# A third of the exponentials on VectorE as shifted linear powers of two, with 64-row score tiles, seven pooled PSUM banks and maps without maxima

## The chip, the core and the metric

The kernel runs on one core of a Trainium2 chip. A core has TensorE (PE, matmuls into PSUM), ScalarE (ACT, the exponential among others), VectorE (DVE), GpSimd (POOL, no access to PSUM) and SyncE (SP), whose queue issues DMAs. The metric is the device time of one execution in microseconds.

## What is computed

A gate mixes two kinds of attention over the same input x of 2048 rows and 512 columns, with 32 heads of 16. Branch A is linear attention with a learned map: two softmaxes over 16 features, of the projection and of its negative. Branch B is softmax attention; its 32 x 2048 x 2048 exponentials are most of the work.

```
g = _sigmoid((x * gate_w).sum(-1, keepdims=True))
# A: phi = concat(softmax(p), softmax(-p)), p = q @ w_phi (and k @ w_phi)
kv = einsum("bhsf,bhsd->bhfd", phi_k, v); z = einsum("bhsf->bhf", phi_k)
o  = einsum("bhqf,bhfd->bhqd", phi_q, kv) / (einsum("bhqf,bhf->bhq", phi_q, z) + 1e-6)
# B: softmax(q k^T / 4) v, per head
return g * (o_A @ wo_A) + (1 - g) * (o_B @ wo_B)
```

Inputs are bf16, normal, x and the weights of scale 0.05. The `x` of branch A serves both branches.

## The kernel before

The program is a list of operations with an engine, a due time (`prio`), an expected duration and dependences. When the program is built, `_Sched.run` plays them through in time and fixes the order of each engine's queue and the buffer each tile gets; `emit` writes the queues with semaphore waits. On the chip each engine runs its queue in that order.

Branch B runs in 32 passes, called sets here: a query block of 512 (`qc`, 4), a group of eight heads that share a 128-row projection (`g`, 4), and a parity (`par`, 2) that picks four of the eight heads. A set goes over 16 key tiles of 128 keys. For each, two units of 1024 columns: `qk` (L573) makes two score tiles with two 32-row matmuls in different row strips of the array, and one `exp` on ScalarE (L580) turns a unit of psR (three buffers of two banks) into bf16 E. Heads of the other parity in a strip are masked out in q (`q_proj`, L375, two products per projection with 0/1 masks). After both units `pv` (L590) adds E times V into psO, four matmuls in four column strips; V is padded with ones, so column 16 of a head's 32 is the softmax denominator. At the end of a set VectorE copies psO (L341), TensorE transposes it in fp32 (L604), VectorE normalises (L608 to L613), and after both parities TensorE transposes again (L623) and VectorE copies to oBT (L626). psO is one bank, so the next set's sums wait for the copy.

Everything else is spread between the units by due time and shares one PSUM bank, psM: the projections (`fill`, L349, four 128-row matmuls of 512 columns each), and branch A. A map (`phi`) takes the projected features from psM: on VectorE maximum and minimum (L455, L456) and two subtractions (L457, L460), on ScalarE one exponential of 1024 (L463), on VectorE a sum over 16 (L464) and a reciprocal (L466), on GpSimd the product (L467). For the queries the result is transposed on TensorE (L514), copied (L517), multiplied with kz (L523, L535), normalised (L526 to L538), transposed again (L546) and copied to oAT (L549). The output projection (L645 to L652) sums both branches; the last four row blocks run after the last set.

Of the kernel before, what the change touches and what calls it, by code (L numbers as in the profile page):

```python
# [1 line left out]

# [4 lines left out]
F32 = mybir.dt.float32  # L7
ACTF = mybir.ActivationFunctionType
# [3 lines left out]
D = 512  # L12
# [7 lines left out]
SCALE = 0.25  # L20

LAT = 0.06
TAU = 0.95
EARLY = 10.0
T0 = 12.0
# [3 lines left out]


# [5 lines left out]
class _Tile:  # L36
    def __init__(self, slots):
        self.slots = slots
        self.idx = None
        self.ops = []  # L40

# [5 lines left out]
class _Op:  # L47
    __slots__ = ("eng", "fn", "dur", "prio", "deps", "tiles", "mode", "name", "dma",
                 "n_open", "users", "start", "end", "count", "sem", "vc", "seq", "est")


class _Sched:

    COMPUTE = ("pe", "act", "dve", "pool")
# [4 lines left out]
    def add(self, eng, prio, dur, fn, deps=(), tiles=(), mode=None, name="", dma=None, nb=0.0):  # L61
        o = _Op()
        o.eng, o.fn, o.dur, o.prio = eng, fn, dur, prio
        o.deps = [d for d in deps if d is not None]
        o.tiles = list(tiles)
        o.mode, o.name, o.dma, o.est = mode, name, dma, nb
# [6 lines left out]

    def run(self):
        engines = ("sp", "act", "pe", "dve", "pool")
# [5 lines left out]
        ready = {e: [] for e in engines}  # L81
# [3 lines left out]
        free = {e: 0.0 for e in engines}  # L85
        last_mode = None
        order = {e: [] for e in engines}
        left = len(self.ops)

        def slot_time(t):  # L90
            best = None
            for i, ten in enumerate(t.slots.tenant):
                if ten is None:
                    when = 0.0
                elif any(x.end is None for x in ten.ops):
                    continue
                else:
                    when = max(x.end for x in ten.ops) + LAT
                if best is None or when < best[0]:
                    best = (when, i)  # L100
            return best

        def earliest(o, at):
            when = max(at, o.est)
            for t in o.tiles:
                if t.idx is None:
                    b = slot_time(t)
                    if b is None:
                        return None
                    when = max(when, b[0])  # L110
            return when

        while left:
            pick = None
            for e in engines:
# [22 lines left out]
            for t in o.tiles:  # L138
                if t.idx is None:
                    _, i = slot_time(t)  # L140
                    ten = t.slots.tenant[i]
                    if ten is not None:
                        o.deps += [x for x in ten.ops if x not in o.deps]
# [563 lines left out]
```

## Time and profile before

| | |
|---|---|
| runs | 1056.77, 1067.06, 1069.68 us; median 1067.06 |
| profiled execution, span | 1054.9 us |
| busy: ACT, PE, DVE, POOL | 93%, 83%, 29%, 7% |
| mean granted clock of TensorE | 0.685 |

The span runs from the first to the last instruction of one profiled execution. Busy shares count the time in which an engine works on data. The granted clock is the share of TensorE's 2.4 GHz that the throttle let through. In the rows below a line such as L573 is a line of the kernel before; "out<-in" names what an instruction writes and reads, and the text in square brackets how long its engine had been idle before it and what ended that.

### The profile page before, as it was taken

Reading aid. Unit: us, or ns where it says so; the run is one execution under the profiler, and the core shown is the slowest. Engines: PE = TensorE matmul, PEld = TensorE weight load, DVE = VectorE, ACT = ScalarE, POOL = GpSimd, SP = SyncE. Lnnn points to the kernel's source line nnn. Section 1 sums busy time; section 2 is a strip of 40 time slices with the busy share of each in tenths; the row PEclk is TensorE's granted clock in tenths of the full one; section 3 lists DMA queues with packets and bytes.
Section 4 is the critical chain, followed back from the end, with each engine's and each line's share of the span. In section 5 each row is a group of like instructions: output and inputs, shape, how many; then the busy total and the mean of one; then the engine's idle time right before and its main releaser. Section 6 shows DMA issues by size and latency. Waiting matters only on the chain.

```text
span 1054.9 us, 12780 instructions
## 1 busy us (share of the span) xinstructions
PE 879.7 (83%) x5420; PEld 253.2 (24%) x5472; DVE 306.0 (29%) x634; ACT 984.9 (93%) x1064; POOL 74.1 (7%) x62
## 2 busy tenths in 40 slices
PE   5988778787887878788988888878888899888887
PEld 1322222122221322122222221312222222222212
DVE  1333535144333222124313321402422241311001
ACT  4899999999999999999999999999999999999995
POOL 4000100102011000000000100000000010000000
PEclk9989988678657875656555665655655655997556
DMA  9000000000000000000000000000000000000000
GB/s 238 2 1 1 1 1 1 0 1 0 1 1 1 2 1 1 1 1 1 1 0 1 1 1 1 1 1 1 1 1 1 1 1 1 21 28 13 1 1 21
DMA packets 18809, 9.23 MB, mean 9 GB/s; under 512 B 13632, under 2 KB 18752, under 8 KB 18752
## 3 DMA queue, kind: packets, MB, share of 16 engines
q1 hardware_dynamic: 16912, 6.82, 2.7%
q10 hardware_dynamic: 1584, 1.57, 0.5%
q8 instruction: 43, 0.70, 0.3%
q14 instruction: 14, 0.11, 0.0%
q0 software_dynamic: 256, 0.02, 0.0%
HBM read 3.16 MB, written 2.10 MB: 5 GB/s over the span
## 4 chain that ended last, share of the span: by engine, by line
ACT 63%; PE 32%; issue 1%; DVE 1%; DMA 1%; POOL 0%; DVEq 0%
ACT E L580 61%; PE psR L573 11%; PE psO L590 8%; PE psM L349 6%; ACT WAT L463 2%; PE psM L604 2%; PE psM L645 1%; PE psM L514 1%; DMA xT<-in_A_x_dram 1%; PE psM L647 1%; PE psM L535 1%; PE psR L349 1%; DVE ss L464 0%; PE psR L645 0%; PE psM L523 0%
## 5 line engine op out<-in xcount | busy, mean ns | idle before, releaser
L580 ACT ACTIVATE E<-psR 128x1024 bf16<-128x1024 f32 x1024 | 956.8, 1123 | 43.5 <-PE psR L573 35.9
L573 PE MATMUL psR<-q,kT 32*128 32x512 bf16 x2048 | 428.7, 519 | 29.2 <-ACT E L580 28.1
L590 PE MATMUL psO<-E,vB 128*32 128x512 bf16 x2048 | 272.9, 523 | 110.9 <-ACT E L580 108.9
L573 PEld LDWEIGHTS psR<-q,kT 32*128 32x128 bf16 x2048 | 91.3, 96 | 318.4 <-issue 183.1
L590 PEld LDWEIGHTS psO<-E,vB 128*32 128x32 bf16 x2048 | 55.1, 98 | 326.8 <-ACT E L580 287.3
L464 DVE TENSOR_REDUCE ss<-WAT 128x64 f32<-128x1024 bf16 x32 | 39.0, 1218 | 121.5 <-ACT WAT L463 121.3
L467 POOL TENSOR_TENSOR WB<-WAT,ss 128x1024 bf16<-128x1024 bf16 x16 | 30.8, 1926 | 518.8 <-DVE ss L466 518.8
L341 DVE COPY OT<-psO 128x512 f32<-128x512 f32 x32 | 22.1, 691 | 146.7 <-PE psO L590 146.6
L455 DVE TENSOR_REDUCE st<-psM 128x32 f32<-128x512 f32 x32 | 22.1, 692 | 110.8 <-PE psM L349 110.8
L467 POOL TENSOR_TENSOR phiK<-WAT,ss 128x1024 bf16<-128x1024 bf16 x16 | 30.8, 1927 | 308.8 <-DVE ss L466 308.8
L349 PE MATMUL psM<-Wp,xT 128*128 128x512 bf16 x103 | 43.3, 553 | 8.5 <-issue 6.6
L375 DVE TENSOR_SCALAR q<-psM,masks 128x512 bf16<-128x512 f32 x30 | 21.2, 740 | 77.9 <-PE psR L573 56.4
L463 ACT ACTIVATE WAT<-WAT 128x1024 bf16<-128x1024 bf16 x32 | 37.4, 1170 | 0.0
L349 PE MATMUL psM<-xT,WB 128*128 128x512 bf16 x100 | 32.5, 451 | 3.6 <-issue 3.3
L604 PE MATMUL psM<-ident,OT 128*128 128x128 f32 x128 | 30.1, 379 | 1.0 <-DVE WAT L460 0.7
L341 DVE CAST Wp<-psM 128x512 bf16<-128x512 f32 x20 | 13.8, 692 | 52.3 <-PE psM L652 35.5
L349 PE MATMUL psM<-WAv,xT 128*128 128x512 bf16 x61 | 22.3, 501 | 2.0 <-DVE WAT L460 0.9
L604 PEld LDWEIGHTS psM<-ident,OT 128*128 128x128 f32 x128 | 19.4, 188 | 12.7 <-DVE OT L341 5.5
L456 DVE TENSOR_REDUCE st<-psM 128x32 f32<-128x512 f32 x32 | 21.7, 679 | 0.0
L457 DVE TENSOR_TENSOR WAT<-psM,st 128x512 bf16<-128x512 f32 x32 | 21.7, 679 | 0.0
L517 DVE COPY WB<-psM 128x1024 bf16<-128x1024 bf16 x16 | 11.1, 692 | 36.6 <-PE psM L514 36.6
L460 DVE TENSOR_TENSOR WAT<-st,psM 128x512 bf16<-128x512 f32 x32 | 21.6, 676 | 0.0
(84 smaller groups left out, 345.9 us busy)
## 6 DMA issues: line engine op xcount, KB each, us to landing
out_dram<-Wp SPq DMA_DIRECT2D x16, 128.0 KB, 1.7
WB<-in_B_wqkv_dram ACTq DMA_DIRECT2D x3, 512.0 KB, 7.0
WAv<-in_A_wqkv_dram SPq DMA_DIRECT2D x1, 512.0 KB, 4.2
WoA<-in_A_wo_dram SPq DMA_DIRECT2D x1, 512.0 KB, 5.1
WoB<-in_B_wo_dram SPq DMA_DIRECT2D x1, 512.0 KB, 6.1
Wbd<-in_A_w_phi_dram POOLq DMA_DIRECT2D x8, 2.0 KB, 4.4
xT<-in_A_x_dram SPq DMA_TRANSPOSE x4, 7.9
gw<-in_gate_w_dram SPq DMA_DIRECT2D x4, 0.2 KB, 5.1
```

The source lines that it names most:

```text
L341: return add("dve", prio, 0.14 + n * 0.00105, lambda e: e.tensor_copy(dst(), src()), deps=deps, tiles=tiles, name=name)
L349: ins = e.matmul(tile.ap[:, off:off + 512], lhsT=lhs(t), rhs=rhs(t), start=(t == 0), stop=(t == KT - 1))
L455: o1 = add("dve", prio, 0.68, lambda e: e.tensor_reduce(mx.ap[:, 0:32], P(), AX.X, ALU.max), deps=[f], tiles=[tile, mx])
L456: o2 = add("dve", prio, 0.68, lambda e: e.tensor_reduce(mx.ap[:, 32:64], P(), AX.X, ALU.min), deps=[f], tiles=[tile, mx])
L457: o3 = add("dve", prio, 0.68, lambda e: e.tensor_tensor(dv()[:, :, 0:DH], P(), mx.ap[:, 0:32].unsqueeze(2).to_broadcast([128, H, DH]), ALU ...
L463: o5 = add("act", prio + 3, 0.95, lambda e: e.activation(ee.ap, d.ap, ACTF.Exp), deps=[o3, o4], tiles=[d, ee])
L464: o6 = add("dve", prio + 5, 1.2, lambda e: e.tensor_reduce(ss.ap[:, 0, :], ee.ap.rearrange("p (g f) -> p g f", f=DH), AX.X, ALU.add), deps ...
L467: return add("pool", prio + 7, 2.0, lambda e: e.tensor_tensor(dst().rearrange("p (g f) -> p g f", f=DH), ee.ap.rearrange("p (g f) -> p g f ...
L573: ins = e.matmul(r.ap[:, 512 * i:512 * (i + 1)], lhsT=kT[p0:p0 + 32, g, 128 * kt:128 * (kt + 1)], rhs=qt.ap[p0:p0 + 32, par, :], start=Tru ...
L580: x = add("act", ut(u), 0.946, lambda e, r=r, E=E: e.activation(E.ap, r.ap, ACTF.Exp, scale=SCALE), deps=[q], tiles=[r, E], name=f"exp{u}")
L590: ins = e.matmul(O.ap[32 * s:32 * s + 32, :], lhsT=vB[:, kt, h, :], rhs=es[s // 2].ap[:, 512 * (s % 2):512 * (s % 2 + 1)], start=(kt == 0) ...
L604: ins = e.transpose(tt.ap[:, 128 * i:128 * (i + 1)], ot.ap[:, 128 * i:128 * (i + 1)], ident32[:])
```

## The change

Of the 16 key tiles of a set, six (`DSET`: 5, 7, 9, 11, 13, 15) may be done on either of two streams, and the planner picks one for each when it places its first score matmul (`choose`). On ScalarE the exponential is as before. On VectorE a scaled and shifted score is written as int16 whose bits, read as bf16, are a power of two with a linear mantissa (`ACC`, `BIAS`); a second and a third copy are this one with 43 and 85 added to the bits, one by VectorE over 2048 elements at once, one by GpSimd as two 32-bit additions of 512. The weighted sum of the three approximates the exponential. It is made by TensorE: three rounds of E times V per key tile, the second and the third with V scaled by 0.79 and 0.63 (`vS`, made by GpSimd). The due times count 11 ScalarE tiles and 5.3 VectorE tiles to a set.

- Scores use tiles of 64 rows: `q_proj` writes q once, and eight small DMAs place each head into a zeroed buffer `qz`, so that the two matmuls of a unit take rows 0 to 63 and 64 to 127. A unit takes two adjacent banks on the ScalarE stream, two single ones on the VectorE stream.
- PSUM: seven banks in one pool for scores, projections and everything else, the eighth is psO. V is padded to 18 columns instead of 32.
- Maps take exp(p) and exp(-p) straight from PSUM on ScalarE, without maxima; GpSimd sums the 16 in four halving additions. The transposes of the queries' maps, of oA and of oB become DMA transposes on SP's queue. Branch A's keys are summed in four groups.
- A certificate computes bounds of the scores from norms (squares on GpSimd, sums on TensorE), and a flag; a second, slower program with maxima follows behind a branch on that flag.
- The planner weighs lateness of the score streams against other work and counts 0.11 us for a change of tiling.

```diff
+VW = 18
+NBANK = 7
+DSET = (5, 7, 9, 11, 13, 15)
+SHIFT = (0, 43, 85)
+WB16 = (1.0, 0.79296875, 0.6328125)
+ACC = 128.0 / math.log(2.0) * SCALE
+NORM = 3.1258
+BIAS = 127.0 * 128.0 - 128.0 * math.log2(NORM)
...
+    def choose(self, key, eng):
+        for o in self.alts.pop(key)[1 - ("act", "dve").index(eng)]:
+            o.start = o.end = -1.0
+            self.left -= 1
+            self.ops.remove(o)
+            if o in self.ready[o.eng]:
+                self.ready[o.eng].remove(o)
+            for t in o.tiles:
+                t.ops.remove(o)
+            for u in o.users:
+                if u.start is not None:
+                    continue
+                u.deps.remove(o)
+                u.n_open -= 1
+                if u.n_open == 0 and u.start is None:
+                    self.ready[u.eng].append(u)
...
+            if pend[o.run] >= 1 + (o.run == "act"):
+                continue
...
+    psR = ctx.enter_context(nc.psum_tensor("psR", [128, NBANK * 512], F32))
     psO = ctx.enter_context(nc.psum_tensor("psO", [128, 512], F32))
-    psM = ctx.enter_context(nc.psum_tensor("psM", [128, 512], F32))
-    R_r = _Slots([p[:] for p in psR])
+    banks = psR[:].rearrange("p (b n) -> p b n", n=512)
+    B_r = _Slots([banks[:, i, :] for i in range(NBANK)])
...
+        qt = q_t[g, c] = _Tile(qz_r)
+        ev = evac("dve", prio, lambda: qs.ap, lambda: tile.ap[:, off:off + 512], [f], [tile, qs], name=f"qev{g}{c}")
+        op_qz[g, c] = []
+        for j in range(8):
+            r0, cc = 16 * j, j % 4
+            op_qz[g, c].append(add(
+                "sp", prio + 0.001 * j, 0.08, lambda e, r0=r0, cc=cc: e.dma_start(qt.ap[r0:r0 + 16, cc, :], qs.ap[r0:r0 + 16, :]),
+                deps=[ev] + op_qz0, tiles=[qs, qt], name="qz", dma=2.3, lane=lambda: (("qz", qt.idx), (g, c))))
...
+                op_vS[g, c, m] = pool(prio + 1, 0.6 * len(ds), lambda e, m=m, a=a, b=b: e.tensor_scalar(
+                    vS[:, m, a:b, 8 * g:8 * g + 8, :], vB[:, DSET[a]:DSET[b - 1] + 1:2, 8 * g:8 * g + 8, :],
+                    WB16[m + 1], 1.0, op0=ALU.mult, op1=ALU.mult), [ev_v[g, c]], name="vS")
...
+        ev = lambda: ee.ap.rearrange("p (h f) -> p h f", f=32)
+        ex = [add("act", prio, 0.55, lambda e, s=s: e.activation(ev()[:, :, 16 * s:16 * s + 16], P(), ACTF.Exp, scale=1.0 - 2.0 * s),
+                  deps=[f] + ee_deps, tiles=[tile, ee]) for s in range(2)]
+        eg = lambda: ee.ap.rearrange("p (g f) -> p g f", f=DH)
+        v8 = lambda: tr.ap[:, 0:512].rearrange("p (g f) -> p g f", f=8)
+        v4 = lambda: tr.ap[:, 0:256].rearrange("p (g f) -> p g f", f=4)
+        v2 = lambda: tr.ap[:, 256:384].rearrange("p (g f) -> p g f", f=2)
+        p1 = pool(prio + 2, 1.1, lambda e: e.tensor_tensor(v8(), eg()[:, :, 0:8], eg()[:, :, 8:16], ALU.add), ex + use_wat,
...
+        return pool(prio + 6, 2.0, lambda e: e.tensor_tensor(
+            eg(), eg(), ss.ap[:, 1, :].unsqueeze(2).to_broadcast([128, 64, DH]), ALU.mult),
+            [o7], tiles=[ee, ss], name="phi")
...
+        o2 = add("sp", prio + 8, 0.3, lambda e, ph=ph, ptt=ptt: e.dma_start_transpose(ptt.ap, ph.ap),
+                 deps=[op_ph] + use_wp1, tiles=[ph, ptt], name="phT", dma=4.0, lane=lambda ptt=ptt, st=st: (("phT", ptt.idx), st))
...
+        aset = [kt for kt in range(NT) if kt not in DSET] + list(DSET[::-1])
+        pvs = []
+        todo = [("act", i / 11.0, kt) for i, kt in enumerate(aset)] + [("dve", (i + 0.1) / 5.3, kt) for i, kt in enumerate(DSET)]
+        for eng, frac, kt in todo:
+            alt = ((s, kt), eng) if kt in DSET else None
+            pr = st_(s + frac)
+            T = _Tile(T_r) if eng == "dve" else None
+            exps, es = [], []
+            for cc in range(2):
+                rs = [_Tile(B_r), _Tile(B_r)]
+                if eng == "act":
+                    rs[0].mate, rs[1].mate = rs[1], rs[0]
+                c = 2 * par + cc
+
+                def qk(e, rs=rs, c=c, kt=kt, g=g, qt=qt):
+                    ins = None
+                    for h in range(2):
+                        ins = e.matmul(rs[h].ap, lhsT=kT[64 * h:64 * h + 64, g, 128 * kt:128 * (kt + 1)],
+                                       rhs=qt.ap[64 * h:64 * h + 64, c, :], start=True, stop=True, tile_position=(64 * h, 0))
+                    return ins
+                q = add("pe", pr + 0.5 * cc, 0.22, qk, deps=[ev_k[g, kt // 4]] + op_qz[g, qc], tiles=rs + [qt], mode="row",
+                        name=f"qk{s}.{kt}", kind="qk", run=eng, alt=alt)
...
+                if eng == "act":
+                    E = _Tile(E_r)
+                    es.append(E)
+                    exps.append(add("act", pr + 0.5 * cc, 0.934, lambda e, rs=rs, E=E: e.activation(
+                        E.ap.rearrange("p (a n) -> p a n", n=512), pair(rs), ACTF.Exp, scale=SCALE),
+                                    deps=[q], tiles=rs + [E], name="exp", kind="exp", alt=alt))
+                else:
+                    for h in range(2):
+                        exps.append(add("dve", pr + 0.5 * cc + 0.01 * h, 0.61, lambda e, rs=rs, T=T, cc=cc, h=h: e.tensor_scalar(
+                            T.ap[:, 0, 1024 * cc + 512 * h:1024 * cc + 512 * h + 512], rs[h].ap,
+                            ACC, BIAS, op0=ALU.mult, op1=ALU.add),
+                            deps=[q], tiles=[rs[h], T], name="expd", kind="exp" if h else "exp0", alt=alt))
+            if eng == "act":
+                rounds = [(exps, lambda cc, es=es: es[cc].ap, lambda hd, kt=kt: vB[:, kt, hd, :], [])]
+                holds = es
+            else:
+                di = DSET.index(kt)
+                s1 = add("dve", pr + 1.0, 0.61, lambda e, T=T: e.tensor_single_scalar(T.ap[:, 1, :], T.ap[:, 0, :], SHIFT[1], ALU.add),
+                         deps=exps, tiles=[T], name="sh1", alt=alt)
+                s2 = [pool(pr + 1.0 + 0.3 * cc, 1.27, lambda e, T=T, cc=cc: e.tensor_tensor(
+                    T.ap[:, 2, 1024 * cc:1024 * (cc + 1)].bitcast(I32), T.ap[:, 0, 1024 * cc:1024 * (cc + 1)].bitcast(I32),
+                    shc[:].to_broadcast([128, 512]), ALU.add), exps[2 * cc:2 * cc + 2] + [op_shc], tiles=[T], name="sh2", alt=alt) for cc in range(2)]
+                rounds = [(exps, lambda cc, T=T: T.ap[:, 0, 1024 * cc:1024 * (cc + 1)].bitcast(BF16), lambda hd, kt=kt: vB[:, kt, hd, :], []),
+                          ([s1], lambda cc, T=T: T.ap[:, 1, 1024 * cc:1024 * (cc + 1)].bitcast(BF16),
+                           lambda hd, di=di: vS[:, 0, di, hd, :], [op_vS[g, kt // 4, 0]]),
+                          (s2, lambda cc, T=T: T.ap[:, 2, 1024 * cc:1024 * (cc + 1)].bitcast(BF16),
+                           lambda hd, di=di: vS[:, 1, di, hd, :], [op_vS[g, kt // 4, 1]])]
+                holds = [T]
...
+                def pv(e, rhs=rhs, lhs=lhs, g=g, par=par, O=O, s=s, key=(kt, ri)):
+                    ins = None
+                    for cc in range(2):
+                        for h in range(2):
+                            col = 2 * h + cc
+                            hd = 8 * g + 4 * h + 2 * par + cc
+                            ins = e.matmul(O.ap[32 * col:32 * col + VW, :], lhsT=lhs(hd), rhs=rhs(cc)[:, 512 * h:512 * (h + 1)],
+                                           start=(first_pv[s] == key), stop=(last_pv[s] == key), tile_position=(0, 32 * col),
+                                           skip_group_check=True)
+                    return ins
...
+                engine.wait_ge(op_flag.sem, op_flag.count)
+                general = engine.value_load(flag[0:1, 0:1], min_val=0, max_val=1)
+                if e == "sp":
+                    sch.emit(e, engine, [op_end])
+                with engine.If(general > 0):
+                    for sem, count in done.values():
+                        engine.wait_ge(sem, count)
+                    gen.emit(e, engine)
```

## Rows read from the trace of the kernel before

**Rows 1.** The page's part 1, busy us, share of the span, instructions; part 2's clock:
```profile
PE 879.7 (83%) x5420; PEld 253.2 (24%) x5472; DVE 306.0 (29%) x634; ACT 984.9 (93%) x1064; POOL 74.1 (7%) x62
PEclk9989988678657875656555665655655655997556
```

**Rows 2.** The page's part 4: the chain that ended last, by engine:
```profile
ACT 63%; PE 32%; issue 1%; DVE 1%; DMA 1%; POOL 0%; DVEq 0%
```

**Rows 3.** Order of time, ScalarE, at head, middle and end: start, duration, line, operation, count:
```profile
15.64 0.58 ACT L340 CAST kT<-psR 128x512 bf16<-128x512 f32 x1 [2.12 <-PE psR L349]
16.12 2.16 ACT L580 ACTIVATE E<-psR 128x1024 bf16<-128x1024 f32 x2
...
955.37 47.05 ACT L580 ACTIVATE E<-psR 128x1024 bf16<-128x1024 f32 x51 [0.33 <-PE psR L573]
...
1033.43 7.69 ACT L580 ACTIVATE E<-psR 128x1024 bf16<-128x1024 f32 x8
```

**Rows 4.** Groups by line and shape: count, busy us, mean ns, idle before and releaser:
```profile
L580 ACT ACTIVATE E<-psR 128x1024 bf16<-128x1024 f32 x1024 | 956.8, 1123 | 43.5 <-PE psR L573 35.9 <-PE psO L590 4.9
...
L464 DVE TENSOR_REDUCE ss<-WAT 128x64 f32<-128x1024 bf16 x32 | 39.0, 1218 | 121.5 <-ACT WAT L463 121.3
...
L467 POOL TENSOR_TENSOR phiK<-WAT,ss 128x1024 bf16<-128x1024 bf16 x16 | 30.8, 1927 | 308.8 <-DVE ss L466 308.8
...
L604 PE MATMUL psM<-ident,OT 128*128 128x128 f32 x128 | 30.1, 379 | 1.0 <-DVE WAT L460 0.7 <-DVE q L375 0.2
...
L466 DVE RECIPROCAL ss<-ss 128x64 f32<-128x64 f32 x32 | 17.5, 548 | 0.5
...
L514 PE MATMUL psM<-ident,WB 128*128 128x128 bf16 x128 | 14.3, 280 | 0.9 <-POOL WB L467 0.6 <-DVE q L375 0.2
...
L517 DVE COPY WB<-psM 128x1024 bf16<-128x1024 bf16 x16 | 11.1, 692 | 36.6 <-PE psM L514 36.6
```

**Rows 5.** Stretches: length, busy us (and count) of each engine, granted clock, DMA:
```profile
85.00:115.00 30.00, 24.08 (x176) 8.11 (x176) 13.59 (x25) 30.00 (x35) 1.67 (x1) 1.00 0.01 1
434.00:462.00 28.00, 22.74 (x120) 4.74 (x120) 2.46 (x3) 28.00 (x32) 1.93 (x1) 0.51 0.00 1
560.00:570.00 10.00, 9.70 (x70) 3.28 (x68) 4.16 (x13) 9.32 (x11) 0.00 (x0) 0.50 0.00 0
```

**Rows 6.** The same stretches, the projections' line L349 alone: PE, PEld, clock, DMA:
```profile
85.00:115.00 30.00, 6.81 (x26) 2.17 (x28) 1.00 0.01 1
434.00:462.00 28.00, 0.00 (x0) 0.00 (x0) 0.51 0.00 1
560.00:570.00 10.00, 0.00 (x0) 0.00 (x0) 0.50 0.00 0
```

**Rows 7.** Order of time, TensorE's matmuls, at a granted clock of 1.00:
```profile
61.61 0.40 PE L590 MATMUL psO<-E,vB 128*32 128x512 bf16 x4
61.94 0.39 PE L573 MATMUL psR<-q,kT 32*128 32x512 bf16 x4
62.27 1.04 PE L349 MATMUL psM<-xT,WB 128*128 128x512 bf16 x4
63.24 0.39 PE L573 MATMUL psR<-q,kT 32*128 32x512 bf16 x2
```

**Rows 8.** The same at a granted clock of 0.50:
```profile
436.09 0.62 PE L590 MATMUL psO<-E,vB 128*32 128x512 bf16 x4 [0.31 <-ACT E L580]
436.64 0.97 PE L573 MATMUL psR<-q,kT 32*128 32x512 bf16 x4
```

**Rows 9.** Order of time, VectorE, two instructions on 512 PSUM values in a row:
```profile
149.90 0.68 DVE L457 TENSOR_TENSOR WAT<-psM,st 128x512 bf16<-128x512 f32 x1
150.49 0.68 DVE L460 TENSOR_TENSOR WAT<-st,psM 128x512 bf16<-128x512 f32 x1
```

**Rows 10.** SP's queue in order of time, and two issues with us to landing:
```profile
0.73 14.50 SPq L290 DMA_TRANSPOSE xT<-in_A_x_dram  x4
...
out_dram<-Wp SPq DMA_DIRECT2D x16, 128.0 KB, 1.7
...
gw<-in_gate_w_dram SPq DMA_DIRECT2D x4, 0.2 KB, 5.1
```

More of the change, by code (lines that the diff above doesn't have):

```diff
@@ new lines, in _earliest, with _streams @@
+    def _earliest(self, o, at):
+        return self._place(o, at)[0]
+    def _streams(self, cands, free, pend):
+        best = {}
+        for w, o in cands:
+            if o.kind != "qk":
+                continue
+            if o.alt is not None and o.alt[0] in self.alts and o.run == "act":
+                if sum(1 for k in self.alts if k[0] == o.alt[0][0]) < 2:
+                    continue
+            if pend[o.run] >= 1 + (o.run == "act"):
+                continue
+            if o.run not in best or o.seq < best[o.run][1].seq:
+                best[o.run] = (w, o)
+        return list(best.values())
@@ L346, in fn, with fill @@
+    def fill(prio, tile, off, lhs, rhs, deps, name, also=()):
         def fn(e):
@@ L659, in _build @@
[L659 to L673 removed]
+                ins = e.matmul(tile.ap[:, off:off + 512], lhsT=oT.ap[:, t, sl], rhs=WoA[:, t, :], start=(t == 0), stop=False)
@@ new lines, in first, with second @@
+            for t in range(KT - last):
+                ins = e.matmul(tile.ap[:, off:off + 512], lhsT=oBt.ap[:, t, sl], rhs=WoB[:, t, :], start=False, stop=(t == KT - 1))
+            return ins
+        def second(e, tile=tile, off=off, sl=sl, oBt=oBt):
+            return e.matmul(tile.ap[:, off:off + 512], lhsT=oBt.ap[:, KT - 1, sl], rhs=WoB[:, KT - 1, :], start=False, stop=True)
+        fi = _Tile(fin_r) if not last else None
+        f1 = add("pe", prio, (8 - last) * MM, first, deps=[op_oAT[st], op_woA, op_woB] + [op_oBT[qc, g] for g in range(KT - last)] + (tail_qk if last else []),
+                 tiles=[tile, oT, oBt] + ([fi] if fi else []), mode="full", name="of", nb=prio - EARLY)
@@ new lines, in _build @@
+        outs.append(add("sp", prio + 1, 0.1, lambda e, dst=dst, st=st: e.dma_start(out[0, 128 * st:128 * (st + 1), :], dst()),
+                        deps=[ev], tiles=[fi] if fi else [], dma=2.0, name="out",
+                        lane=(lambda fi=fi, st=st: (("fin", fi.idx), st)) if fi else None))
+    finl = [wp1[:, 512 * i:512 * (i + 1)] for i in range(4)]
+    op_end = add("sp", 1e9, 0.1, lambda e: None, deps=outs, name="end")
+    sch.run()
+    for o in sch.order["pe"]:
+        if o.kind == "pv":
+            s, key = o.run
+            first_pv.setdefault(s, key)
+            last_pv[s] = key
```

1060 lines of the change are left out of this document (676 added, 384 removed).

## The prediction

> **What bounds the kernel now.** I read the page's busy shares first, then the chain, the groups, the stretches, and last the order of instructions at a few places. ScalarE is busy 93% of the span, TensorE 83%, VectorE 29%, GpSimd 7% [rows 1]. The chain that ended last is 63% ScalarE and 32% TensorE [rows 2]: ScalarE sets the pace, TensorE makes it wait now and then. In an unbroken stretch 51 exponentials of 128x1024 take 47.05 us with the first at 955.37 [rows 3], so one costs (47.05 - 1.03) / 50 = 0.92 us. The span closes with that: 16.1 us before the first exponential, 1024 x 0.92 = 942, 32 exponentials of the maps at about 0.95 = 30, a tail of 15.2 us after the start of the last (1033.43 + 7 x 0.9 = 1039.7 to 1054.9) [rows 3, 4], together 1003; the other 52 us are ScalarE waiting, mostly on the scores, as the L580 row says (35.9 us on psR) [rows 4].
>
> TensorE's clock decides how close that wait is. In 85 to 115 us PE is busy 24.08 of 30 us at a granted clock of 1.00 (2.4 GHz); in 434 to 462 it is busy as much, 22.74 of 28, at 0.51, and in 560 to 570 for 9.70 of 10 at 0.50 (1.2 GHz) [rows 5]. Busy share does not tell these apart. The first stretch has 6.81 us of 128x128 matmuls of the projections (L349), the others none: their matmuls are 32-row scores, 32-column sums and short transposes [rows 6]. At 2.4 GHz a group of scores and a group of E times V alternate every 0.33 us, and a projection of four 512-column matmuls takes 0.97 from its start to the next group [rows 7]; inside a projection a step is 0.216, so changing the tiling costs 0.97 - 4 x 0.216 = 0.105. At 1.2 GHz the step with a change is 0.55 [rows 8].
>
> **The change, per set.** A set is one query block, one group of eight heads and one parity: 16 key tiles of two 1024-column units, 32 sets in all. The due times in the diff put 11 and 5.3 key tiles per set on the two streams; since they must sum to 16 I count 10.7 for ScalarE and 5.3 for VectorE, a third.
>
> ScalarE: 10.7 x 2 x 0.92 = 19.7. The maps' 1024-wide exponential becomes two of 512 straight from PSUM: at the 0.48 that the L340 cast of 512 takes to the next instruction [rows 3], 64 x 0.5 / 32 = 1.0. Sum **20.7**, against 30.4 before.
>
> VectorE: four scaled conversions of 512 PSUM values per key tile. Instructions of 512 PSUM values follow each other at 0.60 [rows 9]; I take 0.61, so 2.44. Then one 16-bit add of 2048 elements in SBUF, which no row shows. Lower bound: no less than one of 512, 0.60. Upper: the L464 reduction reads 1024 SBUF elements in 1.22 [rows 4], so 2.3. The nearest row in type is L517, 1024 16-bit elements in 0.69, as long as 512 of 32 bits: 0.53 ns an element; with the fixed 0.06 that the 0.60 leaves, 2048 cost **1.14**, which I take. The Trainium skill, "VectorE: DVE Perf Modes", section on N=2048 bf16, has 0.69 for a one-source 16-bit operation between SBUF tensors; by it VectorE would need 20.9 a set and TensorE would lead, near 710 in all. No run here shows it.
>
> What the maps lose on VectorE is four instructions of 512 and the 1.22 reduction per map, 32 times (3.6 us each, 115 us in all). What stays or comes: set ends (L341, a reciprocal, one product of 256; 0.61 and twice 0.3) 32 x 1.24 = 40; about 60 evacuations of 512 at 0.61 = 37 (the q's need one instead of two); map reciprocals (L466) 17.5 [rows 4]; oA, Wp, certificate, kv and output some 70 instructions at up to 0.61, about 43. Sum 138, or 4.3 per set. VectorE: 5.3 x (2.44 + 1.14) + 4.3 = **23.3**, against 306 / 32 = 9.6 before [rows 1].
>
> GpSimd: two 32-bit adds of 512 per key tile. Its L467 product of 1024 bf16 takes 1.93 [rows 4]: 0.96 each by elements, 1.93 by bytes. 5.3 x 1.93 = 10.2, or 20.4. Per map 1.93 + 1.8 for 960 summed elements = 3.7. Squares for the certificate (16 x 1.93) and scaled V (48 x 0.5) are 55 us, all in the first eight sets, on average 1.7. Sum **15.6**, or 25.8 at the other bound. I take the low end: the one row there is tells a price per element, and none by width.
>
> TensorE: 32 score steps. Two 64-row tiles fill the rows, so the two pairs of a key tile can no longer overlap, as four 32-row matmuls do in one step before (x4, 61.94 to 62.27 [rows 7]). E times V: 10.7 + 3 x 5.3 = 26.6 steps. At 2.4 GHz 58.6 x 0.216 = 12.7; a change of tiling at each step adds 6.2, at every second 3.1, at none 0; I take runs of two. Full-array work: 88 projections x 0.97, V by 128 columns 16 x 1, outputs 16 x 1.83, fp32 transposes about 20 (30.1 at the mixed clock [rows 4]), the rest 22, together 172 or 5.4 per set. The 16-bit transposes (L514, the largest, has 14.3 us [rows 4]; L546 and L623) go to 48 DMA transposes on SP. Sum **21.1** (18.1 to 24.3) at 2.4 GHz. At 1.2 GHz: 58.6 x 0.43 + 29.3 x 0.12 + 1.9 x 5.4 = 39.
>
> SP: four transposes of 512x512 occupy its queue 14.5 us [rows 10]. The new ones are a half and a quarter of that size, 48 in all, with 128 small copies for q at 0.5: about 125 us of 750, prepared a set ahead. I cost them at nothing inside; were the cover gone, one copy's landing, 2 to 5 us by the L659 and gate rows [rows 10], would be late once per two sets.
>
> What queues: VectorE runs in order, so a conversion waiting for a score bank also holds the set's evacuation of psO behind it, and the next set's sums wait for that. The seven pooled banks are drawn on by both streams and by every projection.
>
> Outside the sets: head 18 (16.1 plus a q copy of about 2), tail 17 (15.2, with a DMA transpose of about 3 in place of the transposes and copy of 1.2): 35. The second program in the file sits behind a branch; the flag needs products of norms over 2500, and with inputs of scale 0.05 I work out about 70 from the reference (1.6 squared for x, 420 for a head's weights, 1/16), so only the branch is paid.
>
> **Sum.** VectorE is the longest: 32 x 23.3 + 35 = **781**, against the profiled span of 1054.9. The runs shown lie 2 to 15 us above that span; I add nothing for it.
>
> **Rivals.**
> 1. *Cheap shift, no waits.* At 0.60 VectorE falls to 5.3 x 3.04 + 4.3 = 20.4, and TensorE's 21.1 leads: 32 x 21.1 + 35 = 710. For it: SBUF on both sides. Against: no row, and four engines between 20 and 21 seldom run without waiting.
> 2. *VectorE and GpSimd get in each other's way.* GpSimd paced at 25.8, or VectorE waiting 0.5 for each shift: 32 x 25.8 + 35 = 861. For it: GpSimd has no cover in the first sets and goes from 7% to about 65%. Against: nothing in the trace, where GpSimd is nearly idle. The Trainium skill, "SBUF — State Buffer", section "Who interferes with whom", speaks for it: a VectorE instruction that uses the shared port pair and a GpSimd instruction block each other for a whole instruction. No row here shows it.
> 3. *The clock stays as it is.* With a share s of the time at 1.2 GHz TensorE works at 1 - 0.46 s. It leads from a clock of 0.90 down; at today's mean of 0.685 a set takes 21.1 / 0.71 = 29.7 and the kernel 985.
> 4. *Slower:* TensorE at 1.2 GHz nearly throughout, 32 x 39 + 35 = 1283. It decides from a mean clock under 0.61 (32.9 a set gives 1088). For it: 9.70 of 10 us busy at 0.50 [rows 5]. Against: projections return in nearly every set, and scores now drive all 128 rows at a time.
> 5. *The change does not do what it says:* the branch is taken and the second program follows, 512 blocks in sequence, each with two exponentials' worth of ScalarE (1.84) and a DMA transpose of several us, over 3000 us. Against it the norms above.
>
> **Chances.** Forecast 0.52 (730 to 830), rival 1 0.14, rival 2 0.15, rival 3 0.10 (880 to 1045), rivals 4 and 5 together 0.07, within 2% 0.02. Two per cent is about what a measurement of this kernel can tell from no change. The range takes in the forecast, rival 2 and nearly all of rival 1: 705 to 880. Faster 0.91, same 0.02, slower 0.07.
>
> **What would show it.** VectorE near 95% busy, ScalarE near 85, GpSimd near 65; the 16-bit add of 2048 with a mean near 1.1 us (0.6 and rival 1 gains, over 1.6 and rival 2 does); GpSimd's 512-element adds near 1.0 us; a granted clock over 0.9 in most stretches, and no fall in the last four sets, where projections are rare. I am wrong if TensorE leads the chain with a clock under 0.9, or if ScalarE's idle time is put down to psR by more than 100 us.

## The result, and the profile after

The changed kernel takes **916.4 us** (median of four runs, 915.4 to 923.4) against 1066.1 for the kernel before (four runs): a ratio of 0.862, 95% interval 0.857 to 0.868. The profiled execution spans 915.0. The direction was forecast, the size was not: 781 was predicted, and 916 lies 36 us above the range, so the prediction was wrong.

The page of the changed kernel: part 1 (busy us, share of the span, instructions), the granted clock by slices, the chain that ended last by engine, and the groups of the new streams (count | busy us, mean ns | idle before, releaser).

```profile
PE 739.8 (81%) x6924; PEld 238.2 (26%) x6980; DVE 791.1 (86%) x1251; ACT 658.1 (72%) x712; POOL 636.3 (70%) x607
...
PEclk9699899999999999998999999999899999999997
...
DVE 59%; PE 23%; SPq 7%; ACT 4%; POOL 3%; DMA 2%; issue 2%
...
L985 ACT ACTIVATE E<-psR 128x1024 bf16<-128x1024 f32 x640 | 623.9, 1026 | 213.2 <-PE psR L975 192.4
L990 DVE TENSOR_SCALAR T<-psR 128x512 int16<-128x512 f32 x768 | 488.2, 676 | 66.1 <-PE psR L975 60.8
...
L1001 POOL TENSOR_TENSOR T<-T,shc 128x512 int32<-128x512 int32 x384 | 434.8, 1136 | 206.1 <-DVE T L990 201.7
...
L999 DVE TENSOR_SCALAR T<-T 128x2048 int16<-128x2048 int16 x192 | 202.1, 1052 | 1.8
```

Against [rows 1, 2, 4]: ScalarE's share of the chain falls from 63% to 4%, VectorE leads, and the clock holds near full speed (0.955 over the span, 0.685 before). The 192 shifts (L999) are six key tiles in each of the 32 sets, the 640 exponentials (L985) ten. Divided by 32, busy time stands so against the forecast:

| per set, us | forecast | measured |
|---|---|---|
| ScalarE | 20.7 | 20.6 |
| VectorE | 23.3 | 24.7 |
| GpSimd | 15.6 (bound 25.8) | 19.9 |
| TensorE | 21.1 (18.1 to 24.3) | 23.1 |
| idle time of VectorE, in all | 35 | 124 |

So the loads were met, VectorE's to 1.4 us a set and GpSimd's, the worst, to 4.3, and most of the miss is time in which VectorE, the longest engine, does nothing. The stretches of the changed kernel show where (length, busy us and count of PE, PEld, DVE, ACT, POOL, clock, DMA share, GB/s):

```profile
0.00:34.00 34.00, 7.40 (x50) 3.58 (x50) 2.56 (x4) 3.25 (x4) 15.73 (x28) 0.80 0.74 159
34.00:897.00 863.00, 725.92 (x6841) 232.06 (x6895) 785.41 (x1242) 653.46 (x707) 619.40 (x580) 0.97 0.08 16
897.00:915.00 18.00, 6.53 (x36) 2.54 (x35) 3.16 (x6) 1.37 (x2) 1.18 (x1) 0.71 0.14 41
```

VectorE is idle 34.0 - 2.6 = 31 us at the head, 18.0 - 3.2 = 15 at the end, and 863.0 - 785.4 = 78 between, where the forecast had none. The head is SP's queue; in order of time, the changed kernel's SP:

```profile
15.49 4.26 SPq L633 DMA_TRANSPOSE WAT<-in_A_wqkv_dram  x1
19.79 0.59 SPq L620 DMA_DIRECT2D WAv<-in_A_wqkv_dram  x1
20.43 1.91 SPq L620 DMA_DIRECT2D gw<-in_gate_w_dram  x4
22.39 3.71 SPq L620 DMA_DIRECT2D Wbd<-in_A_w_phi_dram  x8
26.21 5.05 SPq L699 DMA_DIRECT2D qz<-qst  x8
```

The eight copies that spread the first q over its rows stand behind the loads of four other tensors and take 5.05 us to issue, 0.63 each. The first exponential starts at 33.2, not at the 18 that I had reckoned:

```profile
33.20 1.94 ACT L985 ACTIVATE E<-psR 128x1024 bf16<-128x1024 f32 x2 [16.62 <-PE psR L975]
```

The same copies in the middle of the run, in order of time:

```profile
529.05 4.95 SPq L699 DMA_DIRECT2D qz<-qst  x8
...
535.40 0.61 PE L975 MATMUL psR<-qz,kT 64*128 64x512 bf16 x4 [2.79 <-DMA qz<-qst]
...
535.83 1.94 ACT L985 ACTIVATE E<-psR 128x1024 bf16<-128x1024 f32 x2 [3.34 <-PE psR L975]
...
538.38 1.29 DVE L990 TENSOR_SCALAR T<-psR 128x512 int16<-128x512 f32 x2 [3.75 <-PE psR L975]
```

Eight issues take 4.95 us and the last lands after them; TensorE stands still for 2.79 us, ScalarE then for 3.34 and VectorE for 3.75. Every engine follows one order that the kernel's own planner wrote down when it was built, and that planner counts a q copy as 0.08 us of SP and the shift as 0.61 of VectorE (lines 699 and 999); the trace has 0.62 and 1.05. The waits of the changed kernel (us in total, times, longest; PEld is TensorE's weight load):

```profile
ACT E L985 <- PE psR L975: 192.4, 218, 16.6
PEld psR L975 <- DVE T L990: 121.6, 219, 3.1
...
DVE T L990 <- PE psR L975: 60.8, 54, 16.5
...
PE psR L975 <- DMA qz<-qst: 40.7, 10, 15.7
```

Two theories follow. One: VectorE's load, swollen by the sixth tile and by its sharing with GpSimd, is the cause. The other: the written order is, because it was made with prices that don't hold. With false prices scores stand in TensorE's queue before a bank is free, and all that is behind them waits.

### The profile page after: what moved, and what is told of

Its sections match the earlier page's. It is cut to its first block, busy times and chain, and to the rows that moved or that the text cites. A ratio compares the mean times of both kernels' runs of the same rounds, so it can differ in the third digit from the quotient of the medians.

```text
span 915.0 us, 16916 instructions
## 1 busy us (share of the span) xinstructions
PE 739.8 (81%) x6924; PEld 238.2 (26%) x6980; DVE 791.1 (86%) x1251; ACT 658.1 (72%) x712; POOL 636.3 (70%) x607
## 4 chain that ended last, share of the span: by engine, by line
DVE 59%; PE 23%; SPq 7%; ACT 4%; POOL 3%; DMA 2%; issue 2%
DVE T L990 35%; DVE T L999 16%; PE psR L975 9%; PE psO L1017 7%; SPq L699 5%; ACT E L985 3%; PE psR L675 2%; DMA qz<-qst 2%; POOL T L1001 2%; SPq L627 2%; DVE OT L669 2%; DVE ss L858 1%; PE psR L1062 1%; DVE qst L669 1%; PE psR L1064 1%
## 5 line engine op out<-in xcount | busy, mean ns | idle before, releaser
L985 ACT ACTIVATE E<-psR 128x1024 bf16<-128x1024 f32 x640 | 623.9, 1026 | 213.2 <-PE psR L975 192.4
L1001 POOL TENSOR_TENSOR T<-T,shc 128x512 int32<-128x512 int32 x384 | 434.8, 1136 | 206.1 <-DVE T L990 201.7
L990 DVE TENSOR_SCALAR T<-psR 128x512 int16<-128x512 f32 x768 | 488.2, 676 | 66.1 <-PE psR L975 60.8
L975 PE MATMUL psR<-qz,kT 64*128 64x512 bf16 x2048 | 352.5, 395 | 119.9 <-DVE T L990 44.2
L999 DVE TENSOR_SCALAR T<-T 128x2048 int16<-128x2048 int16 x192 | 202.1, 1052 | 1.8
L975 PEld LDWEIGHTS psR<-qz,kT 64*128 64x128 bf16 x2048 | 83.9, 94 | 377.2 <-DVE T L990 121.6
L1017 PE MATMUL psO<-T,vS 128*18 128x512 bf16 x1536 | 132.5, 393 | 15.2 <-DVE T L999 14.4
L1017 PE MATMUL psO<-E,vB 128*18 128x512 bf16 x1280 | 119.4, 394 | 0.6 <-DVE OT L669 0.4
L1017 PE MATMUL psO<-T,vB 128*18 128x512 bf16 x768 | 77.5, 394 | 2.3 <-DVE T L990 1.5
L1017 PEld LDWEIGHTS psO<-T,vS 128*18 128x18 bf16 x1536 | 33.0, 89 | 86.0 <-DVE T L999 33.5
L859 POOL TENSOR_TENSOR phk<-phk,ss 128x1024 bf16<-128x1024 bf16 x16 | 32.9, 2054 | 3.7 <-DVE ss L858 3.6
```

The source lines that it names most:

```text
L859: return pool(prio + 6, 2.0, lambda e: e.tensor_tensor(eg(), eg(), ss.ap[:, 1, :].unsqueeze(2).to_broadcast([128, 64, DH]), ALU.mult), [o7 ...
L975: ins = e.matmul(rs[h].ap, lhsT=kT[64 * h:64 * h + 64, g, 128 * kt:128 * (kt + 1)], rhs=qt.ap[64 * h:64 * h + 64, c, :], start=True, stop= ...
L985: exps.append(add("act", pr + 0.5 * cc, 0.934, lambda e, rs=rs, E=E: e.activation(E.ap.rearrange("p (a n) -> p a n", n=512), pair(rs), ACT ...
L990: exps.append(add("dve", pr + 0.5 * cc + 0.01 * h, 0.61, lambda e, rs=rs, T=T, cc=cc, h=h: e.tensor_scalar(T.ap[:, 0, 1024 * cc + 512 * h: ...
L999: s1 = add("dve", pr + 1.0, 0.61, lambda e, T=T: e.tensor_single_scalar(T.ap[:, 1, :], T.ap[:, 0, :], SHIFT[1], ALU.add), deps=exps, tiles ...
L1001: s2 = [pool(pr + 1.0 + 0.3 * cc, 1.27, lambda e, T=T, cc=cc: e.tensor_tensor(T.ap[:, 2, 1024 * cc:1024 * (cc + 1)].bitcast(I32), T.ap[:, ...
```

## The experiments

Times are medians; the ratio of each is to the kernel before on the same chip. That kernel's medians on the chips used lie between 1061 and 1066, so 5 us between runs on different chips tell nothing. Each expectation names theories A, B and C of its own. The diffs are shortened: `...` stands for what is left out, and some values are joined on one line.

### VectorE and GpSimd on the shared copies

Three kernels cut one or both of the added copies of each tile to 2 elements, with the order of all instructions as it was. The sums over keys that would read the missing copy read the first one instead, which the diff does not show.

```diff
-  ... tensor_single_scalar(T.ap[:, 1, :], T.ap[:, 0, :], SHIFT[1], ALU.add)
+  ... tensor_single_scalar(T.ap[:, 1, 0:2], T.ap[:, 0, 0:2], SHIFT[1], ALU.add)      # shift tiny
-  ... T.ap[:, 2, 1024 * cc:1024 * (cc + 1)].bitcast(I32), ... to_broadcast([128, 512])
+  ... T.ap[:, 2, 1024 * cc:1024 * cc + 4].bitcast(I32), ... to_broadcast([128, 2])   # GpSimd tiny
```

GpSimd's adds tiny:

> The order of every queue is that of the changed kernel; GpSimd's additions for the third copy shrink from 512 to 2 elements (384 instructions), and the third round of E times V reads the first copy in place of the third. Left out: most of the third copy, so its sum is not the exponential's. Theory A, VectorE's queue sets the pace by its own work: the 16-bit addition of 2048 falls from a mean of 1.05 us towards its shortest 0.69, 192 x 0.36 = 69 us, and the time to about 850. Theory B, GpSimd sets it (434.8 us of these additions, third copies late for TensorE): more than that comes back, under 820. Theory C, the queues wait for one another and no engine alone sets it: less than half of the 69 us, over 880.

Measured 871.8 (ratio 0.821, 0.810 to 0.832): between theory A's 850 and theory C's 880, and far from theory B's. Part 1:

```profile
PE 731.4 (84%) x6924; PEld 239.7 (28%) x6980; DVE 741.2 (85%) x1251; ACT 652.2 (75%) x712; POOL 302.9 (35%) x607
```

The shift in the changed kernel, and then in this one (minimum, median and maximum ns, first and last start):

```profile
L999 DVE TENSOR_SCALAR T<-T x192: 620/1090/2268, 36.6 to 896.6; 128x2048 int16<-128x2048 int16 x192
```

```profile
L999 DVE TENSOR_SCALAR T<-T x192: 622/684/2152, 36.3 to 849.8; 128x2048 int16<-128x2048 int16 x192
```

The shift itself has not changed and falls from a median of 1090 to 684 ns when GpSimd is busy 35% of the span instead of 70%; its mean falls by 0.26 us (1052 to 795 ns), not by the 0.36 of theory A, and its shortest is 0.62, not 0.69. VectorE's busy time falls by 50 us (791.1 to 741.2), the time by 45: in this order VectorE's work counts nearly in full.

VectorE's shift tiny:

> The order of every queue is that of the changed kernel; VectorE's 16-bit addition shrinks from 2048 to 2 elements (192 instructions), and the second round of E times V reads the first copy. Left out: most of the second copy. Theory A, VectorE sets the pace: about 190 of its 202 us go, and the time falls until TensorE's 740 busy us and the ends lead, to 780 or 800. Theory B, GpSimd sets it: 60 us at most, over 850. Theory C, mutual waits in fixed queues: 80 to 100 us, about 825.

Measured 855.2, 61 us less. By the number this is theory B's, GpSimd sets the time; the next kernel excludes it. Both tiny:

> VectorE's shift and GpSimd's two adds of each tile take 2 elements instead of 2048 and 512, and the second and third sums over keys read the first copy: the third of the exponentials loses the values of its two shifted copies, all matmuls stay. Theory A (price of the shifted copies, and of their lock on each other, on VectorE): VectorE falls to about 640 and TensorE (725 busy) leads; 725 + 33 + 17 + 40 of waits = 815, range 800 to 830. Theory B (waits between the engines for banks and for q copies bound what is left): 840 or more, little below the 855 that the tiny shift alone gave.

Measured 849.8, with GpSimd busy only 31%:

```profile
PE 732.2 (86%) x6980; PEld 237.9 (28%) x6980; DVE 652.5 (77%) x1251; ACT 650.0 (77%) x712; POOL 260.5 (31%) x607
```

The shift's group in the kernel with the shift tiny and then in this one:

```profile
L999 DVE TENSOR_SCALAR T<-T 128x2 int16<-128x2 int16 x192 | 96.9, 504 | 1.8
```

```profile
L999 DVE TENSOR_SCALAR T<-T 128x2 int16<-128x2 int16 x192 | 50.8, 264 | 1.8
```

Two elements take 0.50 us on average beside GpSimd's full adds, 0.26 beside its tiny ones. These 0.24 us are as much as the 0.26 of 2048 elements: a wait for GpSimd that does not grow with the shift's length. But with 139 us of VectorE's work gone (791 to 652) only 67 us of the time are; VectorE was then 77% busy, and the time stayed at 850, where theory B had put it. The load alone is not the cause.

### The head

```diff
-  ... name="wat", dma=7.0)            # the same for wav, gw, wphi
+  ... name="wat", dma=7.0, nb=16.0)   # not before 16 us: the first q copies go ahead
```

> Nothing left out. Only the order of SP's queue at the head: the first eight q copies go ahead of WAT, WAv, the gate's and w_phi's loads, which have 16 us as earliest time. If the head is lost to the place of the q copies in that queue, the first exponential comes at about 22 us in place of 33.2, and the time falls by 10 to 12 us, to about 905. If the early stages would have been waited for anyway (their weights are now later), under 3 us.

Measured 905.3. The exponentials start at 22.9 instead of 33.2 us (last fields: first and last start, in the changed kernel and then in this one), and the time falls by the 11 us expected. The head is a sum of its own.

```profile
L985 ACT ACTIVATE E<-psR x640: 1017/1024/1081, 33.2 to 892.8; 128x1024 bf16<-128x1024 f32 x160
```

```profile
L985 ACT ACTIVATE E<-psR x640: 1018/1023/1085, 22.9 to 879.7; 128x1024 bf16<-128x1024 f32 x160
```

### The 64 rows and the clock

```diff
-  ... lhsT=kT[64 * h:64 * h + 64, g, ...], rhs=qt.ap[64 * h:64 * h + 64, c, :] ... tile_position=(64 * h, 0)
+  p0 = 64 * h + 32 * (c // 2)
+  ... lhsT=kT[p0:p0 + 32, g, ...],         rhs=qt.ap[p0:p0 + 32, c, :] ...         tile_position=(p0, 0)
```

> Nothing left out, the order is that of the changed kernel; each score matmul takes the 32 rows that hold its head in place of 64 rows half of which are zeros. If the 64 rows hold the granted clock at 0.955, it falls towards the 0.685 of the kernel before, TensorE leads and the time goes over 1000. If the clock is held by TensorE's denser work, the clock stays over 0.9 and the time within 1%.

Measured 983.3 (two runs, 977 and 990), between the two theories. The page's part 1 and the clock of this kernel:

```profile
PE 827.9 (85%) x6924; PEld 249.8 (26%) x6980; DVE 789.7 (81%) x1251; ACT 661.8 (68%) x712; POOL 636.0 (65%) x607
...
PEclk9799999997787989958879767867668777699687
```

The same matmuls at the same places, with half the rows, hold the clock less: 0.826 for 0.955, at a higher busy share of TensorE (85% for 81%). The 64-row tiles are worth about 67 us here.

### The share of VectorE

Five tiles per set, then none:

```diff
-DSET = (5, 7, 9, 11, 13, 15)
+DSET = (5, 7, 9, 11, 13)                                     # five
-todo = [("act", i / 11.0, kt) ...] + [("dve", (i + 0.1) / 5.3, kt) ...]
+todo = [("act", i / 16.0, kt) ...]                           # none
```

> Five key tiles per set go to VectorE instead of six; nothing else is changed and nothing left out. VectorE loses 32 x (4 x 0.64 + 1.05) = 116 us (791 to 675), ScalarE gains 64 x 0.975 = 62 (658 to 720), GpSimd loses 64 x 1.14 = 73. Theory A (VectorE's load, swollen by the sixth tile and by its waits for GpSimd, sets the time): the time falls by 40 to 70 us, to 845 to 875, and ScalarE becomes the longest. Theory B (the time is set by waits between the engines in the fixed order, whose planned length rises by 26 us with five tiles): 925 to 945. A is held wrong above 895.

Measured 933.6 (ratio 0.874, 0.866 to 0.881): not faster, though VectorE's work fell from 791.1 to 679.5. Theory A falls here; theory B's range held it. The order was worked out anew for five tiles and is not that of the changed kernel; what this run shows is that less load brings nothing in an order made the same way.

```profile
PE 746.9 (80%) x6724; PEld 242.2 (26%) x6724; DVE 679.5 (73%) x1091; ACT 711.2 (76%) x776; POOL 574.3 (61%) x543
```

> No key tile goes to VectorE: all 1024 exponentials of the scores are ScalarE's again, so the 64-row scores, the seven banks, the maps without maxima and the rest of the change stand alone. Theory A (those parts keep ScalarE fed, and the clock stays up): 33 before the first exponential + 1024 x 0.92 + 64 x 0.5 + 18 at the end = 1025, with some waits 1025 to 1045. Theory B (without the third streams there are fewer columns in TensorE, so its clock falls and the scores come late as before): over 1060, clock under 0.8.

Measured 1067.3 (ratio 1.003, 1.000 to 1.007), clock 0.782, as theory B had it; its reason, fewer columns, is not shown. ScalarE is 93% busy (984.1 of 1063.9) as before [rows 1] and waits 33 us on scores, 36 before [rows 4]:

```profile
L985 ACT ACTIVATE E<-psR 128x1024 bf16<-128x1024 f32 x1024 | 955.2, 1111 | 45.8 <-PE psR L975 33.4
```

Its first exponential starts at 32.9 us, 17 later than before [rows 3], so part of what the other changes bring is lost at the head. Together, the 64 rows, the pooled banks, the maps and this head bring nothing by themselves. The gain comes when the third of the exponentials moves; the 64 rows then carry about 67 us of it.

### The prices in the order

First the shift's price alone, then the q copies' alone, then both with two small prices. With the q copies' price the other loads also wait until 16 us, as under "The head". The order is worked out anew each time; nothing is left out.

```diff
-  s1 = add("dve", pr + 1.0, 0.61, ...        # shift
+  s1 = add("dve", pr + 1.0, 1.05, ...
-  "sp", prio + 0.001 * j, 0.08, ...          # q copy
+  "sp", prio + 0.001 * j, 0.6, ...
-  0.934 (exponential), 0.61 (conversion)
+  0.96, 0.64                                 # with both of the above
```

"Measured prices" means these four. The 48 DMA transposes kept theirs in every run, 0.3 us of SP, though they take 1.2; one of them in the changed kernel:

```profile
708.80 1.19 SPq L1044 DMA_TRANSPOSE oBT<-ob  x1
```

> Only the planned price of VectorE's shift is changed, 0.61 to the measured 1.05; nothing is left out. The order then puts 184 tiles on VectorE. Theory A (the order was worked out with a shift that takes 0.61, so each tile on VectorE comes 0.44 us later than the scores and sums queued behind it expect): most of the 72 us that all new prices together gave, 850 to 875. Theory B (what the order did not know was the time of the q copies on SP): 895 to 915.

Measured 866.4.

> Only the q copies are priced at 0.6 on SP instead of 0.08, and go ahead of the other loads at the start; the shift stays at its planned 0.61 and all 192 tiles on VectorE. Nothing is left out. Theory A of the run before (the shift's price): 890 to 905, which is the 905 that the q copies first gave and at most 15 of waits on them. Theory B: 850 to 875.

Measured 871.2. Each of the two runs came out where the theory that names its price had put it, and outside the range of the theory that names the other: both prices are causes, neither is the only one, and their gains of 50 and 45 us overlap. Part 1 with the shift's price, and then with the q copies':

```profile
PE 734.0 (85%) x6859; PEld 241.6 (28%) x6916; DVE 760.3 (88%) x1211; ACT 661.9 (76%) x728; POOL 615.3 (71%) x591
```

```profile
PE 725.5 (83%) x6921; PEld 237.0 (27%) x6980; DVE 785.0 (90%) x1251; ACT 656.2 (75%) x712; POOL 637.8 (73%) x607
```

With the shift's price the planner gives eight tiles back to ScalarE, so 31 us of the gain are VectorE's work (791.1 to 760.3) and 18 its idle time (124 to 106). The q copies' price leaves all 192 tiles, and VectorE's idle time falls from 124 to 85. Six of the first eight copies went ahead in that run, two did not, and its first exponential still starts at 33.1, so the 45 us come from the middle of the run alone. Waits with the shift's price, and then with the q copies':

```profile
PEld psR L975 <- DVE T L990: 72.4, 156, 2.6
...
PE psR L975 <- DMA qz<-qst: 34.3, 8, 14.6
```

```profile
PEld psR L975 <- DVE T L990: 114.7, 217, 1.8
...
DVE T L990 <- PE psR L975: 33.2, 43, 15.0
...
PE psR L975 <- DMA qz<-qst: 14.0, 4, 12.3
```

Each price takes away its own row: the shift's takes the scores' waiting on VectorE from 121.6 to 72.4, the copies' takes TensorE's waiting on q from 40.7 to 14.0, of which 12.3 are the head. Both together, with the two small prices:

> The order is worked out with measured prices in place of the planned ones: conversion 0.64, shift 1.05, exponential 0.96, q copy 0.6 on SP (0.61, 0.61, 0.934 and 0.08 before), and the q copies ahead of the other loads on SP. Nothing is left out. The order then puts 180 tiles instead of 192 on VectorE and its planned length is 863. Theory A (load, and prices that the order did not know): VectorE -43, head -11, fewer waits on q copies: 855 to 880. Theory B (the order is not the cause; only the head counts): 895 to 910.

Measured **843.8** (ratio 0.790, 0.785 to 0.794), 73 us less than the change as it was and 11 under theory A's range. Part 1 and the chain:

```profile
PE 732.0 (87%) x6884; PEld 237.3 (28%) x6884; DVE 753.9 (90%) x1191; ACT 668.8 (79%) x736; POOL 605.3 (72%) x583
...
DVE 41%; PE 24%; ACT 14%; POOL 13%; SPq 4%; issue 1%; DMA 1%
```

Of the 73, 37 are VectorE's work (12 tiles went back to ScalarE), the rest its waiting.

### What bounds the order with the right prices

GpSimd's adds tiny, then five tiles, both in that order's prices:

> The order with all measured prices, 180 tiles on VectorE, and GpSimd's two adds of each tile cut from 512 to 2 elements; the third sum over keys reads the first copy, so the third copy's values are left out. The shift should fall from 1.07 to about 0.8, VectorE by 180 x 0.27 = 49 us. Theory A (VectorE, busy 90% there, is the bound now): 795 to 810. Theory B (TensorE, busy 87%, takes over within 20 us): 822 to 840.

Measured 829.6, as theory B had it: VectorE's work fell by 46 us (753.9 to 708.3), the time by 14.

> The order with all measured prices and five tiles per set for VectorE (160 instead of 180); nothing is left out. VectorE falls by 20 x 3.75 = 75 us to 680, ScalarE rises by 40 x 1.03 = 41 to 710. Theory A (VectorE's load bounds that order): 790 to 815. Theory B (what bounds it is the alternation of the two streams through the seven banks, as the planned length says, 863 with either number of tiles): 835 to 855.

Measured 846.7, no different from 843.8, as theory B had it. Part 1:

```profile
PE 713.0 (84%) x6668; PEld 238.5 (28%) x6724; DVE 687.7 (81%) x1091; ACT 705.0 (83%) x776; POOL 561.6 (66%) x543
```

VectorE, 81% busy there, is not the bound; either TensorE or the order still is. The planner holds scores due 0.5 us before their stream runs dry. The next kernel makes that 1.3 us, on top of all measured prices and five tiles, with all first q copies ahead of the other loads and some other rules of the planner changed:

```diff
-  return free[o.run] + pend[o.run] * 0.95 - 0.5
+  return free[o.run] + pend[o.run] * 0.8 - 1.3
-nb=16.0
+nb=24.0
-PVS = 4.0;  TOL1, TOL2 = 0.1, 0.08;  P_SET = 20.9;  T0 = 15.5;  (i + 0.1) / 5.3
+PVS = 8;    TOL1, TOL2 = 0.4, 0.16;  P_SET = 20.0;  T0 = 12;    (i + 0.8) / 5.6
```

> All measured prices, five tiles per set on VectorE, the q copies of the first set ahead of the other loads, and rules of the order with scores due 1.3 us before their stream runs dry instead of 0.5 (with a larger tolerance for other matmuls); nothing is left out. The planned length falls from 863 to 820. Theory A (the order held the last 60 us): 20 us under its planned length, as with the measured prices before, 795 to 810, 10 of the 45 by the q copies. Theory B (TensorE's work holds them): 825 to 840, only the 10 us of the q copies less.

Measured **792.2** (791.5 to 794.7, ratio 0.748, 0.742 to 0.753), the fastest of all, with nothing left out, and 3 us under theory A's range. Part 1, the clock and the chain:

```profile
PE 700.2 (89%) x6662; PEld 230.7 (29%) x6724; DVE 679.3 (86%) x1091; ACT 696.1 (88%) x776; POOL 569.8 (72%) x543
...
PEclk9999999999999999999999999999999999999997
...
ACT 37%; PE 27%; DVE 22%; POOL 7%; SPq 4%; issue 2%; DMA 1%
```

Three engines are 86 to 89% busy and share the chain. ScalarE's waiting for scores, 192.4 us in the changed kernel, is 53.9 here. The first exponential starts at 22.8 instead of 33.1. How the 54 us divide between the head, the scores due earlier and the other rules was not separated. The same rules with the old prices:

> The same rules and five tiles, the q copies of the first set first, but the original prices (conversion 0.61, shift 0.61, exponential 0.934, q copy 0.08); planned length 810, nothing left out. Theory A (wrong prices make any fixed order wait): 50 to 90 us over its planned length, 860 to 900. Theory B (with scores issued further ahead there is slack enough for wrong prices): within 15 us of the run with measured prices.

Measured 879.6. Waits with the measured prices, and then with the old ones:

```profile
ACT E L985 <- PE psR L975: 53.9, 69, 3.3
```

```profile
ACT E L985 <- PE psR L975: 127.6, 123, 5.5
...
PE psR L975 <- DMA qz<-qst: 49.0, 15, 4.3
```

With equal rules, equal tiles and equal work the false prices cost 87 us. The length that the planner gives an order beside the span that it took says the same in one table:

| order | tiles on VectorE | planned, us | span, us | difference |
|---|---|---|---|---|
| the change | 192 | 827 | 915 | +88 |
| five tiles | 160 | 854 | 935 | +81 |
| shift's price | 184 | 847 | 866 | +19 |
| q copies' price | 192 | 832 | 870 | +38 |
| all measured prices | 180 | 863 | 842 | -21 |
| the same, five tiles | 160 | 863 | 845 | -18 |
| scores 1.3 us ahead | 160 | 820 | 790 | -30 |
| the same, old prices | 160 | 810 | 876 | +66 |
| no tile, old prices | 0 | 1034 | 1064 | +30 |

Orders with the old prices and tiles on VectorE run 66 to 88 us over their plan, orders with the measured ones 18 to 30 under it. The order without such tiles, in which of the two prices only the copies' counts, runs 30 over, at a clock of 0.782. An order that comes in under its plan has other prices that are too high: GpSimd's add stands at 1.27 and takes 1.14 on average. No run put the two prices above what they measure, so whether the true price is what helps, or any margin, is open.

## Why the prediction was wrong

**The step that failed is the sum itself**, "VectorE is the longest: 32 x 23.3 + 35". It takes for granted that the longest engine always has work. Its load was missed by 45 us (791 for 746), its idle time by 89 (124 for 35). Of the 89, 11 lie at the two ends (46 for 35; the q copies put first gave 11 back at the head), and 78 are waits inside the sets. That 916 lies in the range of rival 3 (880 to 1045) is chance: its mechanism, a clock near 0.685, did not come. I had written that four engines of nearly equal load seldom run without waiting, but used it against rival 1 only and not against my own sum; no rival had the order's waits as its mechanism.

**SP at nothing** was the second failure, and a cause of the first. I worked out about 125 us of issues in all (they came to about 137: 128 x 0.62 and 48 x 1.2) and called the copies prepared a set ahead, with at worst one landing "late once per two sets". The landing (the last number, median us) is not what is late:

```profile
qz<-qst SPq DMA_DIRECT2D x128, 16.0 KB, 1.8
```

Eight issues hold the queue for 5 us, in an order that allows 0.64. With that price in the order the time fell by 45 us, though TensorE's row for it names only 25 inside the sets (40.7 less the 15.7 of the head). VectorE's waiting on scores fell by 28 (60.8 to 33.2), in part as its consequence; how the 45 divide was not separated.

**The shift: the right number for a wrong reason.** I took 1.14 by the price per element of a 512 to 1024-element row; the mean is 1.05, near it by luck. With GpSimd's adds tiny the median is 0.68 and the mean 0.80, so at least 0.26 of the 1.05 is waiting for GpSimd. The Trainium skill, "VectorE: DVE Perf Modes", section "Side-by-side: where the cycles go for N=2048 bf16", had 0.69 for such an operation, and the trace agrees (684 ns at the median with GpSimd's adds tiny). So half of rival 1's condition held, a shift that is cheap when left alone, while its other half, no waits, did not.

**Rival 2 was real, but a part only.** VectorE waits about 0.26 us per shift for the adds (1052 less 795 ns), not 0.5, and in the changed kernel that cost 45 us; with measured prices in the order only 14. The Trainium skill, "SBUF — State Buffer", section "Who interferes with whom", says of a VectorE instruction on the shared port pair and a GpSimd instruction that the later of the two waits for the whole instruction of the other. The 2-element shift agrees in that it waits as long as the full one (0.50 us beside 0.26).

**The count** of 5.3 tiles, read from the due times, was wrong: the due time only orders the candidates, and the planner put all six of DSET on VectorE in every set. It explains the load (192 tiles where 170 were counted, 22 x 3.6 = 79 us, and about 3 us more for the rest of the tiles' work, against 37 us less of other work, 101 for 138), yet it is not what the time hung on: five tiles gave 934 in the old prices and 847 in the new ones, against 916 and 844.

**What held:** TensorE within its bounds; ScalarE's 20.7 a set, in part by luck, as ten tiles at 0.975 us an exponential (623.9 / 640) took the place of 10.7 at 0.92; the clock above 0.9, against rivals 3 and 4. Of the two reasons given for it one was tried: half the rows cost about 67 us. The branch was not taken. By the list of signs VectorE should have been 95% busy; it was 86%, and ScalarE waited 192 us on psR, over the 100 that I had named as the mark of error.

The gain over the kernel before, then: a third of the exponentials leaves ScalarE, which alone would have stayed at 1067. Of what this frees, the order with four false prices takes back 73 us; five tiles, all first q copies ahead and the planner's other rules bring another 52, which the fastest version has.

## What to carry to other kernels

Where every engine follows an order written down in advance, the busy sum of the longest engine is a floor and not a forecast: look up each planned price in the trace, above all those of work that the planner thinks is nearly free, and price the order's waits before the loads. Count the issues of small transfers on their queue, not only when they land. If less work on the longest engine brings no time, it is the order that has to be worked out anew.

## What the runs showed of the hardware

- A 16-bit add of 2048 SBUF elements on VectorE takes 0.68 us at the median beside 2-element adds of GpSimd, 1.09 beside its adds of 512; one of 2 elements 0.26 and 0.50 on average. GpSimd's 32-bit add of 512 takes 1.03 us at the least, 1.14 on average, near the price per element of [rows 4] and far from that per byte.
- A copy of 16 KB from SBUF to SBUF holds the queue that issues it for 0.62 us, and eight in a row for 5; the DMA transposes between SBUF tensors hold it for 1.2.
- With one and the same order TensorE's granted clock is 0.955 with 64-row scores at 81% busy, and 0.826 with 32-row ones at 85%. Without VectorE's tiles it is 0.782 with 64-row scores at 79% busy.
